# A gated convolution and token MLP on one Trainium2 core: kv transform with a butterfly over even and odd rows, halves in another order, more sums by accumulating DMAs

## Chip, core and metric

The kernel runs on one core of a Trainium2 chip. The metric is device time in microseconds (us). "Before" is the kernel without the change. Names of engines: TensorE (PE) does matmuls and writes PSUM; PEld in a profile is its weight loads. VectorE (DVE), ScalarE (ACT) and GpSimd (POOL) compute on SBUF; SyncE (SP) issues most DMAs, ACT issues four small ones and POOL the accumulating ones.

## The reference

Sequence length S = 2048, width D = 640, hidden width F = 1536, all bfloat16:

```python
x = A_q
g = sigmoid((x * gate_w).sum(-1, keepdims=True))
k_shift[s] = sum over t in 0..3 of k[s - 3 + t] * shift_k[:, 3 - t]
kv = k_shift * v
y = irfft(rfft(pad(kv)) * rfft(pad(ssm_k)))[:S] + kv * ssm_D     # causal convolution over s
a = q * y
h = layernorm(x over D)
u = gelu(einsum("sd,sf->df", h, w1) + b1)
b = (einsum("df,fs->ds", u, w2) + b2).T
out = g * a + (1 - g) * b
```

## The kernel before

**Convolution.** The sequence is cut into two halves of 1024 rows. ssm_k and kv are transformed half by half by matmuls against a table of sines and cosines, `FTB`. A half is split into four phases p (row = 4m + p), and each phase is a transform over 256 values of m, two blocks kt of 128 partitions. Its output has two frequency blocks k2 and two components c. `fwd` (line 832) does one phase: for each (k2, c) a group of four matmuls (two kt, two chunks ci of 320 columns) accumulates in PSUM, and ScalarE evicts 640 columns. `mixing` (846) joins the four phases with VectorE sums and differences. `C[0]` and `C[1]` hold the transforms of the two kernel halves (V0, V1 after `mixing` and `v1mix`), `C[2]` and `C[3]` those of kv (A0, A1). `cross` (1089) forms A0 times V1 in V1's place, `product` (1062) A0 times V0 and A1 times V0, `acc_dma` (1070) adds A0 V1 onto A1 V0. `invmix` (1104) undoes the mixing and `inverse(h, Z)` (1123) transforms back with the transposed table `GTB`, multiplies by the gate on eviction and by q on VectorE, adds the MLP's share in `O1` and stores.

**Rows.** ssm_k comes with the channel on the partitions and is turned by TensorE (`transp`, 818, one group per phase and kt). k is turned by a DMA transpose (`k_turn`); `kv` (949) does the 4-tap convolution as banded matmuls.

**MLP.** The first layer ("m1") is 12 tiles ft of 32 matmuls, in groups of 8 per 512 rows hk; its w1 chunks lie in `ring`. The second ("m2") is four blocks of 512 rows in the order `HORD` (1021), each with four groups of 24 matmuls; its `W2` tiles reuse the ring, two alternating, so a block's weights can be loaded only when the block before last is done.

**Order.** The code writes no order by hand. Every operation is handed to a planner (`_Sched.add`, 353) with an estimated duration and a priority (its index unless given); `run` (383) simulates the engines and picks, per engine, the ready operation with the smallest priority, and `emit` issues in that order. Convolution groups and MLP groups share four PSUM slots (at most three and two). m1 has priority 10^6 and up, m2 2x10^6, so MLP groups fill gaps. In `add`, what an evictor depends on is also made a dependence of its group's first matmul. Each engine and each DMA queue then runs its list in order, with semaphore waits where the tracker (`_Tracker`) finds an overlap in memory. The mixing of the kernel halves has priority `MIXP` = 330.

**Aliases that matter.** `wT` lies on C[2]; `ssm`, `vkv0` and `v1` on C[3]; `q_lo` on C[1] slots 2 and 3; `q_hi` on KF and its neighbours; `gq` (the gate's products) on GTB; `cgb` (the inverse's result) on FTB; `tm` and `kv1` on KT.

**End.** `cross(0)`, `cross(1)`, the products for the second half, `invmix`, `inverse(1)`; then a sign change of half of GTB (`neg`), the products of A0 and V0, `invmix`, `inverse(0)`. The last m2 group is joined to the output by VectorE straight from PSUM (`last_stt`).

## Time and profile before

| | us |
|---|---|
| median of 8 runs (lowest to highest) | 191.35 (191.03 to 192.12) |
| the profiled execution | 191.3 |
| its span, first to last instruction | 189.5 |
| 384 + 384 MLP matmuls of 320 columns, busy | 54.1 + 53.1 |
| 64 evictions of transforms (128x640), ScalarE | 39.6 |
| 12 accumulating DMAs on POOL's queue: 2752 packets, 6.55 MB | 20.2% of 16 DMA engines |
| all SP loads and stores: 34464 packets, 32.15 MB | 55.6% |

How to read it: times in the profile are from one execution; its span leaves out 1.8 us of the time measured for that execution. A matmul's profiled duration includes its way through the array, and consecutive ones overlap. A group line gives output and input tiles (buffer numbers left out), shapes, count, busy time and the mean of one in ns. Almost all TensorE, ScalarE and VectorE work has the line of a helper (293, 666, 622), so groups are told apart by tiles and shapes.

### The profile page before, as it was taken

The numbers are of one execution on the slowest core, as the hardware profiler recorded it, in microseconds if no ns is written. First come the engines' busy times: TensorE is split into PE (matmuls) and PEld (weight loads), VectorE is DVE, ScalarE is ACT, GpSimd is POOL, SyncE is SP. The second block draws the span as 40 slices with busy tenths as digits, with TensorE's granted clock in tenths as the row PEclk, the third lists the DMA queues.
The fourth block names the chain that finished last, engine by engine and source line by source line (L and its number), as shares of the span: only waits on it lengthen the run. The fifth ranks groups of instructions, "written<-read, shape, count | busy, mean of one in ns | idle before, by whom it ended". The sixth has DMA issues, their size and how long they took to land.

```text
span 189.5 us, 3367 instructions
## 1 busy us (share of the span) xinstructions
PE 176.5 (93%) x1403; PEld 131.7 (70%) x1403; DVE 170.8 (90%) x197; ACT 116.2 (61%) x185; POOL 33.4 (18%) x33
## 2 busy tenths in 40 slices
PE   0479998979999999999999999999999999999994
PEld 0446575648767886677777777888888777877783
DVE  7999968994999999999999999999999999994253
ACT  4997989899989999997412221131322487337430
POOL 2199021850004510000011303250000000000000
PEclk9999999999999999999999999999999999999999
DMA  4999999993999999996368954999947903400222
GB/s 152 393 394 347 393 237 218 309 401 135 132 191 359 224 156 183 297 317 198 72 142 230 238 100 150 274 208 191 263 136 234 368 16 134 142 2 0 73 104 104
DMA packets 37295, 38.93 MB, mean 205 GB/s; under 512 B 15643, under 2 KB 32672, under 8 KB 37280
## 3 DMA queue, kind: packets, MB, share of 16 engines
q1 hardware_dynamic: 34464, 32.15, 55.6%
q0 software_dynamic: 2752, 6.55, 20.2%
q8 instruction: 11, 0.18, 0.4%
q14 instruction: 4, 0.03, 0.0%
q10 hardware_dynamic: 64, 0.01, 0.0%
HBM read 25.87 MB, written 2.62 MB: 150 GB/s over the span
## 4 chain that ended last, share of the span: by engine, by line
PE 88%; ACT 8%; DMA 3%; issue 0%; DVE 0%
PE pp L293 88%; DMA ssm<-in_A_ssm_k_dram 3%; ACT C L666 3%; ACT wT L666 2%; ACT FTB L666 1%; ACT L666 1%; ACT cw L666 0%; ACT GT L666 0%; DVE O L678 0%
## 5 line engine op out<-in xcount | busy, mean ns | idle before, releaser
L293 PE MATMUL pp<-X,ring 128*128 128x320 bf16 x384 | 54.1, 299 | 0.0
L293 PE MATMUL pp<-GT,W 128*128 128x320 bf16 x384 | 53.1, 299 | 0.0
L293 PEld LDWEIGHTS pp<-GT,W 128*128 128x128 bf16 x384 | 43.6, 113 | 8.7
L622 DVE TENSOR_TENSOR C<-C 128x2560 bf16<-128x2560 bf16 (+1 forms) x28 | 48.9, 1770 | 0.0
L293 PEld LDWEIGHTS pp<-X,ring 128*128 128x128 bf16 x384 | 37.4, 98 | 14.4
L666 ACT ACTIVATE C<-pp 128x640 bf16<-128x640 f32 x64 | 39.6, 729 | 3.2 <-PE pp L293 3.2
L666 ACT ACTIVATE O<-pp,c,omg 128x640 bf16<-128x640 f32 x15 | 13.3, 884 | 27.7 <-PE pp L293 27.7
L262 POOL DMA_DIRECT2D C<-C x10 | 11.0, 1195 | 71.6 <-DVE C L622 40.2
L666 ACT ACTIVATE GT<-pp,cc 128x640 bf16<-128x640 f32 x12 | 9.6, 798 | 22.2 <-PE pp L293 22.1
L293 PE MATMUL pp<-wT,FTB 128*128 128x320 bf16 x128 | 20.2, 313 | 1.2 <-ACT C L666 1.1
L666 ACT ACTIVATE cgb<-pp,gg 128x640 bf16<-128x640 f32 x16 | 12.7, 794 | 11.1 <-PE pp L293 11.0
L293 PEld LDWEIGHTS pp<-wT,FTB 128*128 128x128 bf16 x128 | 11.7, 102 | 8.8 <-ACT C L666 3.3
L622 DVE TENSOR_TENSOR tm<-C,C 128x2560 bf16<-128x2560 bf16 (+1 forms) x8 | 16.9, 2148 | 0.0
L293 PE MATMUL pp<-ident,ssm 128*128 128x128 bf16 x80 | 8.3, 265 | 9.0 <-DMA ssm<-in_A_ssm_k_dram 7.2
L622 DVE TENSOR_TENSOR C<-tm 128x2560 bf16<-128x2560 bf16 (+1 forms) x12 | 14.9, 1263 | 0.1
L293 PEld LDWEIGHTS pp<-ident,ssm 128*128 128x128 bf16 x80 | 6.6, 128 | 10.6 <-DMA ssm<-in_A_ssm_k_dram 7.2
L293 PE MATMUL pp<-C,GTB 128*128 128x320 bf16 x96 | 13.9, 299 | 0.0
L876 DVE BATCH_NORM_STATS2 stats<-X 128x6 f32<-128x320 bf16 x32 | 13.3, 452 | 0.0
L666 ACT ACTIVATE gq<-gq 128x640 bf16<-128x640 bf16 x16 | 11.9, 763 | 0.4 <-DVE gq L622 0.4
L293 PEld LDWEIGHTS pp<-C,GTB 128*128 128x128 bf16 x96 | 9.0, 98 | 4.2 <-ACT O L666 0.3
L622 DVE TENSOR_TENSOR tm<-C,SS 128x5120 bf16<-128x5120 bf16 x4 | 11.2, 2817 | 0.0
L666 ACT ACTIVATE wT<-pp 128x640 bf16<-128x640 f32 x16 | 10.2, 710 | 0.6 <-PE pp L293 0.4
(65 smaller groups left out, 178.6 us busy)
## 6 DMA issues: line engine op xcount, KB each, us to landing
ring<-in_B_w_dram SPq DMA_DIRECT2D x12, 512.0 KB, 12.0
W<-in_B_w_dram SPq DMA_DIRECT2D x8, 768.0 KB, 7.0
C<-C POOLq DMA_DIRECT2D x6, 640.0 KB, 9.5
ssm<-in_A_ssm_k_dram SPq DMA_DIRECT2D x4, 640.0 KB, 9.5
X<-in_A_q_dram SPq DMA_DIRECT2D x4, 640.0 KB, 8.8
kn<-in_A_k_dram SPq DMA_DIRECT2D x4, 640.0 KB, 8.5
out_dram<-O SPq DMA_DIRECT2D x7, 320.0 KB, 2.3
vkv<-in_A_v_dram SPq DMA_DIRECT2D x2, 640.0 KB, 5.1
```

The costliest lines, as they stand in the source:

```text
L262: ins = engobj.dma_start(out_ap, in_ap, accum_op=ALU.add, max_dma_last_dim=2560)
L293: ins = self.nc.tensor.matmul(ps_ap, lhsT=lhsT, rhs=rhs, start=start, stop=stop, skip_group_check=True)
L622: o_ = SC.add(eng, d, lambda s: T.op(eng, lambda e: e.tensor_tensor(o, a, b, op), [a, b], [o]), [a, b], [o], prio=prio, name="tt")
L666: return T.op("ACT", lambda e: e.activation(o, src, func, **kw), rr + [src], ww)
L876: ops.append(SC.add("DVE", 0.38, (lambda o, i: lambda s: T.op("DVE", lambda e: e.bn_stats(o, i), [i], [o]))(o, i), [i], [o]))
```

## The change

**Rows and table.** k and v are loaded with row = 8q + 4kt + p in a half, so kt is the parity of m and no longer its block. The table's frequencies in block k2 = 1 are those of k2 = 0 shifted by 512. ssm_k is loaded in five DMAs by half and channel block (the whole first half ahead of X), and turned in groups of eight transposes per channel block, stride 8, evicted as 1024 columns.

**Even phases.** For kv's phases 0 and 2, `fwd_even` transforms even and odd rows apart, for k2 = 0 only, into a staging area (C[1] slots 0 and 1 for the first half, C[2] slots 0 and 1 for the second), and three VectorE operations form both frequency blocks as sums and differences.

**Sums by DMA.** In the second half's mixing one sum, in the products of A0 one sum each, and in the first half's inverse the four sums with `O1` are made by DMAs with an adding write, issued on POOL's queue.

**Order.** The half finished first is the first: HORD is (0, 1, 2, 3), and `inverse(0)` comes before `inverse(1)`. `q_hi` holds products' temporaries before it holds q. The transposed table is put back into FTB with even and odd rows interleaved (`gil`), the inverse reads it there, and `neg` is gone. Planner figures: the DMA rate goes from 320 to 365 (transposes of k from 170 to 200), a POOL-issued DMA's end is put 3 us later and its bytes halved, and the last m2 group no longer waits in the plan for what its evictor needs (`keep`).

```diff
-                    if d.vt is not vt:
+                    if d.vt is not vt and not vt.keep:
...
-                    op.end = dma_free + 2.0 + (3.0 if e == "POOL" else 0.0)
+                    op.end = dma_free + 2.0 + (6.0 if e == "POOL" else 0.0)
...
-        cgb = [alloc(f"cgb{i}", [128, 2, D], BF16, at=base_of(FTB) + 2560 * i) for i in range(3)]
+        cgb = [alloc(f"cgb{i}", [128, 2, D], BF16, at=base_of(GTB) + 2560 * i) for i in range(3)]
...
-        def ssm_load(hk):
-            dma(ssm[:, :, 512 * hk:512 * hk + 512], dr(A_ssm_k, 512 * hk, [[S, 128], [128 * S, ND], [1, 512]]), 128 * ND * 1024, chain=True)
+        def ssm_load(h, a, b):
+            dma(ssm[:, a:b, 1024 * h:1024 * h + 1024], dr(A_ssm_k, 128 * S * a + 1024 * h, [[S, 128], [128 * S, b - a], [1, 1024]]), 128 * (b - a) * 2048, chain=True)
+
+        def row8(t, hk):
+            return dr(t, (1024 * (hk // 2) + 4 * (hk % 2)) * D, [[8 * D, 128], [1, 4 * D]])
+
+        def kcol(hk):
+            return 16 + 128 * (1 - hk % 2)
...
-            dma(kn[hk % 2][:, :, :], dr(A_k, 512 * hk * D, [[4 * D, 128], [1, 4 * D]]), 128 * 5120, chain=True)
+            dma(kn[hk % 2][:, :, :], row8(A_k, hk), 128 * 5120, chain=True)
...
-            dma(dst, dr(A_v, 512 * hk * D, [[4 * D, 128], [1, 4 * D]]), 128 * 5120, chain=True)
+            dma(dst, row8(A_v, hk), 128 * 5120, chain=True)
...
+        SSM0 = ((0, 1), (1, 3), (3, 5))
+        SSM1 = ((0, 2), (2, 5))
...
-        ssm_load(0)
-        x_load(0)
-        ssm_load(1)
-        for hk in range(1, 4):
+        for a, b in SSM0:
+            ssm_load(0, a, b)
+        for hk in range(4):
             x_load(hk)
-        ssm_load(2)
-        ssm_load(3)
+        for a, b in SSM1:
+            ssm_load(1, a, b)
...
-        iota(acol[:, :, :], [[512, 2], [1, 4]], 0, 4)
-        iota(brow[:, :, :], [[2, 2], [4, 128]], 1, 0)
+        iota(acol[:, :, :], [[4, 2], [1, 4]], 0, 8)
+        iota(brow[:, :, :], [[-512, 2], [4, 128]], 1, 0)
...
-        def transp(h, p, kt):
+        def transp(h, db):
             vt = _VT("cv")
             items = []
-            hk = 2 * h + kt
-            dfold = hk == 0 and p == 0
-            if dfold:
-                for lo, hi in ((0, 512), (512, 640)):
-                    items.append(((lambda s, lo=lo, hi=hi: s[:, lo:hi]), ident[0:1, :], Drow[0:1, lo:hi], True, False))
-            for db in range(ND):
-                items.append(((lambda s, db=db: s[:, db * 128:db * 128 + 128]),
-                              V(ssm, db * S + 512 * hk + p, [[4, 128]]), ident[:, :], not dfold, True))
+            for kt in range(2):
+                for p in range(4):
+                    o = (lambda s, j=4 * kt + p: s[:, 128 * j:128 * j + 128])
+                    dfold = h == 0 and kt == 0 and p == 0
+                    if dfold:
+                        items.append((o, ident[0:1, :], Drow[0:1, 128 * db:128 * db + 128], True, False))
+                    items.append((o, V(ssm, db * S + 1024 * h + 4 * kt + p, [[8, 128]]), ident[:, :], not dfold, True))
             mms(vt, items, name="wtr")
-            act(wT[:, hk, p, :], full, ACT.Copy, vt=vt, name="wT")
+            act(V(wT, 2 * h * SL + 128 * db, [[SL, 2], [D, 4], [1, 128]]), (lambda s: s[:, :].rearrange("q (a b c) -> q a b c", a=2, b=4)), ACT.Copy, vt=vt, name="wT")
...
+        def fwd_even(src, h, dst, Th, Ts):
+            pos = {(0, 0, 0): 0, (0, 0, 1): 1, (0, 1, 0): 2, (0, 1, 1): 3, (2, 0, 1): 4, (2, 1, 0): 5, (2, 1, 1): 6, (2, 0, 0): 7}
+            for p in (0, 2):
+                for kt in range(2):
+                    for c in range(2):
+                        vt = _VT("cv")
+                        items = [(chk(ci), FTB[:, p, kt, c, 0, :], src(kt, p, ci), True, True) for ci in range(2)]
+                        mms(vt, items, name="A")
+                        act(V(Th, Ts * SL + D * pos[(p, kt, c)], [[320, 2], [1, 320]]), two, ACT.Copy, vt=vt, name="Ae")
+
+            def t4(o, n, dims):
+                return V(Th, Ts * SL + D * o, dims + [[1, n]])
+            tt_("DVE", V(dst, 0, [[2 * D, 2], [1, D]]), t4(0, 2 * D, []), t4(2, 2 * D, []), ALU.add)
+            tt_("DVE", V(dst, 2 * SL + 2 * D, [[-2 * D, 2], [1, D]]), t4(4, 2 * D, []), t4(6, 2 * D, []), ALU.add)
+            tt_("DVE", V(dst, D, [[2 * SL, 2], [2 * D, 2], [1, D]]), t4(0, D, [[4 * D, 2], [D, 2]]), t4(2, D, [[4 * D, 2], [D, 2]]), ALU.subtract)
...
-            for p in PORD:
-                for kt in range(2):
-                    transp(h, p, kt)
+            for db in range(ND):
+                transp(h, db)
...
-        for p in PORD:
-            fwd(lambda kt, p, ci: vkv0[:, kt, p, 320 * ci:320 * ci + 320], 0, p, C[2], p, 1.0, "A")
+        SC.add("POOL", 0.3, lambda s: T.op("POOL", lambda e: e.tensor_copy(KT[1][:, :, 15:16], KT[0][:, :, 143:144]), [KT[0][:, :, 143:144]], [KT[1][:, :, 15:16]]),
+               [KT[0][:, :, 143:144]], [KT[1][:, :, 15:16]])
+        srcA = lambda kt, p, ci: vkv0[:, kt, p, 320 * ci:320 * ci + 320]
+        fwd_even(srcA, 0, C[2], C[1], 0)
+        for p in (1, 3):
+            fwd(srcA, 0, p, C[2], p, 1.0, "A")
         mixing(C[2], C[1], 0)
         for hk in range(2, 4):
             kv(hk)
-        for p in PORD:
-            fwd(lambda kt, p, ci: kv1[:, kt, p, 320 * ci:320 * ci + 320], 1, p, C[3], p, 1.0, "A", lambda c, k2: k2 == 1)
-        mixing(C[3], C[2], 0)
+        srcB = lambda kt, p, ci: kv1[:, kt, p, 320 * ci:320 * ci + 320]
+        fwd_even(srcB, 1, C[3], C[2], 0)
+        for p in (1, 3):
+            fwd(srcB, 1, p, C[3], p, 1.0, "A")
+        def mixing_acc(R, Th, Ts):
+            def sl(h, s, n=1):
+                return V(h, s * SL, [[1, n * SL]])
+
+            def pr(h, s, rev=False):
+                return V(h, s * SL + (1280 if rev else 0), [[-1280 if rev else 1280, 2], [1, 1280]])
+            for i in range(2):
+                tt("DVE", sl(Th, Ts + i), sl(R, i), sl(R, 2 + i), ALU.subtract)
+                dma(pr(R, i), pr(R, 2 + i), 128 * 5120, stream="POOL", prio=0, accum=True)
+            tt("DVE", sl(R, 2), sl(R, 0), sl(R, 1), ALU.add)
+            tt("DVE", sl(R, 3), sl(R, 0), sl(R, 1), ALU.subtract)
+            tt("DVE", V(R, SL, [[-1280, 2], [1, 1280]]), pr(Th, Ts), pr(Th, Ts + 1, True), ALU.add)
+            tt("DVE", V(R, 0, [[3 * 1280, 2], [1, 1280]]), pr(Th, Ts), pr(Th, Ts + 1, True), ALU.subtract)
+
+        mixing_acc(C[3], C[2], 0)
...
-        HORD = (2, 3, 0, 1)
+            act(V(FTB, 1024 * p, [[1, 2], [256, 4], [2, 128]]), V(GTB, 1024 * p, [[512, 2], [128, 4], [1, 128]]), ACT.Copy, prio=10 ** 5, name="gil")
+
+        HORD = (0, 1, 2, 3)
         lastvt = []
-        for kt in range(2):
-            dma(q_hi[:, kt, :, :], dr(A_q, (1024 + 512 * kt) * D, [[4 * D, 128], [1, 4 * D]]), 128 * 5120)
         for n_, hk in enumerate(HORD):
             W2h = W2[n_ % 2]
...
+                        vt.keep = True
...
-        A1 = {0: (C[3], 2), 1: (C[2], 0)}
+        A1 = {0: (C[3], 2), 1: (C[3], 0)}
...
+        npr = [0]
+
+        def product(dst, a, v, late=False):
             tt("DVE", P2(T0), P2(a), P2(v), ALU.mult)
+            if late:
+                n_ = npr[0] % 2
+                npr[0] += 1
+                tt("DVE", V(q_hi, n_ * SL, [[1280, 2], [1, 1280]]), H(a, 1), H(v, 0), ALU.mult)
+                tt("DVE", H(dst, 1), H(a, 0), H(v, 1), ALU.mult)
+                tt("DVE", H(dst, 0), H(T0, 0), H(T0, 1), ALU.subtract)
+                dma(H(dst, 1), V(q_hi, n_ * SL, [[1280, 2], [1, 1280]]), 128 * 5120, stream="POOL", prio=0, accum=True)
+                return
...
-                tmp = V(C[3], 1280 * (n_ % 4), [[1, 1280]])
+                tmp = V(q_hi, 1280 * (n_ % 4), [[1, 1280]])
...
-                                items.append((chk(ci), GTB[:, p, kt, c, k2, :], V(hz, sz * SL + (2 * c + k2) * D + 320 * ci, [[1, 320]]),
+                                items.append((chk(ci), V(FTB, 1024 * p + 512 * c + 256 * k2 + 128 * kt, [[1, 128]]), V(hz, sz * SL + (2 * c + k2) * D + 320 * ci, [[1, 320]]),
...
+                qv = (q_hi if h == 0 else q_lo)[:, :, p, :]
+                tt("DVE", qv if h == 0 else cg[:, :, :], cg[:, :, :], qv, ALU.mult)
...
+                elif h == 0:
+                    dma(ov, qv, 128 * 2560, stream="POOL", prio=0, accum=True)
+                    dma(dr(out, (1024 * h + p) * D, [[4 * D, 128], [512 * D, 2], [1, D]]), ov, 256 * 1280, sem="out")
...
-        cross(0)
-        cross(1)
-        y1(0)
-        y1(1)
-        Z1 = invmix(A1[0], A1[1], C3a, None, None)
+        for g in range(2):
+            cross(g)
+        for g in range(2):
+            product(A0[g], A0[g], V0[g], True)
+        for kt in range(2):
+            dma(q_hi[:, kt, :, :], dr(A_q, 512 * kt * D, [[4 * D, 128], [1, 4 * D]]), 128 * 5120)
+        for g in range(2):
+            product(A1[g], A1[g], V0[g])
+            acc_dma(A1[g], V1[g])
+        for kt in range(2):
+            dma(q_lo[:, kt, :, :], dr(A_q, (1024 + 512 * kt) * D, [[4 * D, 128], [1, 4 * D]]), 128 * 5120).after.add(w2last)
+        Z0 = invmix(A0[0], A0[1], C3a, None, None)
+        inverse(0, Z0)
+        Z1 = invmix(A1[0], A1[1], (SS, 0), None, None)
         inverse(1, Z1)
-        for p in (0, 2, 1, 3):
-            gk = GTB[:, p, :, :, 1, :]
-            act(gk, gk, ACT.Copy, scale=-1.0, name="neg")
-        for kt in range(2):
-            dma(q_lo[:, kt, :, :], dr(A_q, 512 * kt * D, [[4 * D, 128], [1, 4 * D]]), 128 * 5120).after.add(w2last)
-        product(A0[0], A0[0], V0[0])
-        product(A0[1], A0[1], V0[1])
-        Z0 = invmix(A0[0], A0[1], (SS, 0), None, None)
-        inverse(0, Z0)
```

## The prediction

> **What bounds the kernel now.** I read the busy shares first, then the chain that ended last in order of time, then a table of busy time by stage, then the two busiest engines as timelines. The shares leave two candidates:
>
> ```profile
> PE 176.5 (93%) x1403; PEld 131.7 (70%) x1403; DVE 170.8 (90%) x197; ACT 116.2 (61%) x185; POOL 33.4 (18%) x33
> ```
>
> The chain decides between them. Its last pieces (start, length, what); the two before them are TensorE from 42.03 and 0.03 of issue:
>
> ```profile
> 46.42 19.40 PE pp L293 x192
> 65.82 0.03 issue
> 65.84 89.23 PE pp L293 x680
> 155.07 0.01 issue
> 155.08 31.74 PE pp L293 x232
> 186.82 0.02 issue
> 186.84 0.55 DVE O L678
> ```
>
> From 42 us to 186.8 us TensorE never waits, so the end is set by the sum of its matmuls. How near VectorE is shows by stage (first length, then busy PE, PEld, DVE, ACT, POOL, clock, DMA share, GB/s):
>
> ```profile
> 14.50:43.20 28.70, 26.95 (x203) 17.45 (x202) 26.21 (x54) 26.09 (x43) 13.18 (x9) 1.00 1.04 319
> 43.20:83.20 40.00, 39.95 (x395) 29.96 (x393) 36.69 (x28) 38.40 (x68) 5.10 (x4) 1.00 1.00 211
> 83.20:116.90 33.70, 33.70 (x251) 24.29 (x249) 33.67 (x33) 11.84 (x24) 3.46 (x4) 1.00 0.67 167
> 116.90:148.40 31.50, 31.50 (x235) 26.31 (x233) 31.43 (x17) 8.76 (x10) 4.87 (x4) 1.00 0.93 232
> ...
> 170.50:187.00 16.50, 16.30 (x121) 12.65 (x118) 7.06 (x12) 7.42 (x9) 0.00 (x0) 1.00 0.19 67
> ```
>
> The clock is full throughout. VectorE is full from 43 to 170.5 us, so it is the second bound, but it ends early. The timelines, VectorE's last butterflies first and then TensorE after them, show by how much:
>
> ```profile
> 167.67 2.89 DVE L622 TENSOR_TENSOR SS<-C,C 128x2560 bf16<-128x2560 bf16 x2
> ```
>
> ```profile
> 171.43 2.34 PE L293 MATMUL pp<-SS,GTB 128*128 128x320 bf16 x16
> 173.60 3.42 PE L293 MATMUL pp<-GT,W 128*128 128x320 bf16 x24
> 176.86 2.34 PE L293 MATMUL pp<-SS,GTB 128*128 128x320 bf16 x16
> 179.03 7.77 PE L293 MATMUL pp<-GT,W 128*128 128x320 bf16 x56
> ```
>
> When VectorE has finished the last butterflies (about 170.5), TensorE still has 80 MLP matmuls that need nothing more from it.
>
> **Matmuls removed.** In each half, `fwd` for phases 0 and 2 issues 2 x 4 groups x 4 = 32 matmuls; `fwd_even` issues 8 groups x 2 = 16. Two halves lose 32. The profiled mean of 299 ns is latency, not pace. The pace is start to start: 28 kv-transform matmuls begin at 52.78 and the next group at 56.62, 3.84/28 = 137 ns; 248 matmuls from 83.19 to 116.88 give 136 ns. 32 x 0.1365 = **4.37 us**, inside the stretch that sets the end. ScalarE evicts 8 groups of 640 columns as before, so it gains nothing; it is 96% busy from 43.2 to 83.2, and TensorE stays dense there only because MLP matmuls fill in. By 83 us, 17 of the 48 first-layer groups of 8 are done and 31 are left, so filler does not run out.
>
> **A new wait.** `fwd_even` parks its partial sums in C[1] slots 0 and 1 (first half) and C[2] slots 0 and 1 (second). So even-phase evictions can start only when mixing of C[1] ends (64.1 us in the trace), and then that of C[2] (80.7). Before, the first half's transform began at 52.78. Queued behind on TensorE: nothing if the planner knows the wait, and it does, because an evictor's dependences are passed to the group's first matmul. In that gap TensorE can do the odd phases (32 x 0.137 = 4.4), the second half's convolution (4.3) and MLP groups at 1.09 each, 10 us of cover for 52.8 to about 62.5. VectorE waits for 8 evictions at about 0.61 (7 in 4.28), 4.9 us, less the two kv products and gate products that fit there: 0 to 3 us lost, I take 1.5. Those are VectorE's, not yet TensorE's.
>
> **VectorE.** Steps by start: 1.40 for 128x2560 (34.69 to 37.50 for two), 2.74 for 128x5120, 0.74 for 128x1280. Added: two butterflies of 2 x 0.74 + 1.40 = 5.8. Removed: one 5120 sum in the second mixing, with the 5120 difference becoming two of 2560 (-2.7); in each product of A0, one 5120 product becomes two of 2560 (+0.06) and one 2560 sum goes (-2.7 for two); four 1280 sums of the inverse (-3.0). Net -2.6: the last butterflies would end near 168, with the new wait 169.5, while TensorE ends at 186.8 - 4.4 = 182.4. After them TensorE needs at least 32 inverse matmuls (4.4), so VectorE can lose 182.4 - 4.4 - 169.5 = 8.5 us more before TensorE stands idle.
>
> **Eight more accumulating DMAs**: two of mixing, two of the A0 products (655 KB each), four in the inverse (328 KB each), 3.9 MB. Nearest rows (KB each, us to landing):
>
> ```profile
> W<-in_B_w_dram SPq DMA_DIRECT2D x8, 768.0 KB, 7.0
> C<-C POOLq DMA_DIRECT2D x6, 640.0 KB, 9.5
> ...
> C<-SS POOLq DMA_DIRECT2D x2, 640.0 KB, 16.2
> ```
>
> So 9.5 to 16.2 us late; I take 10. After the two mixing sums VectorE has the rest of `cross` (four rounds of about 3.6 us) and two products (7 us each) to do, over 20 us; after the products, those of A1 (16 us). Both cover 16. The inverse's sums go to the half finished first, and its stores sit on SP behind them, some 15 us before the end. Here a rule speaks against: the Trainium skill ("SBUF — State Buffer", "A bandwidth-pool intuition that's wrong") says GpSimd can't write descriptors while VectorE holds the shared port: 620 ns become 3100. If that came on top, each pair of sums would land 5 us later, at 15 to 21 instead of 10 to 16, and the mixing pair would just come out from under its cover: some 1 us of VectorE, still inside its slack, 187.0 either way, but a second pair late by as much would be rival (b). The rows were mostly taken beside a full VectorE (33.67 of 33.70 us), so they hold that wait already. I go by the rows: 0.
>
> **Kernel transposes.** Same 80, now with a stride of 8 elements (16 bytes) in the stationary operand instead of 4, and evicted as 10 of 1024 columns instead of 16 of 640. Row: 15 weight loads in 0.97 us, 65 ns each. The same page ("Door 1: The DMA port swizzle") says SBUF lines are 16 bytes and an access in a new line each time pays. By the row it costs 0, a sum of 187.0; by the rule, if the load doubles, 80 x 65 ns = 5.2 us of TensorE and at most 192.2, of which the stage up to 43.2 has room for most (28.7 us, with 158 x 0.1365 + 45 x 0.065 = 24.5 of pace in them). A gain is not excluded (fewer evictions: the 128x1024 form takes 1.035 against 0.710, so 10.4 against 11.4), and the first load is 262 KB instead of 655 KB, 1 us earlier at 393 GB/s. Against it: no kernel transform can begin before all five groups of its half are evicted, where it began after two: some 0.7 us of ScalarE bubble per half. And X lands up to 1.6 us later, behind the first half's 1.31 MB, in front of a VectorE that is busy until 8. Sum of this stage: -1.5 to +2, I take 0.
>
> **The rest, at nothing.** `gil`: four 128x1024 copies, nearest row 1.14 each, 4.6 on ScalarE after 93 us, against 2.5 for `neg` removed; ScalarE then waits 2.4 to 3.6 us at a time for TensorE. Without that cover 4.6. The q load of the half finished first moves on SP from 67.7 us to behind the A0 products' DMAs: W2 loads, the second q load and stores stand behind it. If it waits too long, the second MLP layer waits for W2. `keep` and HORD move only groups that are ready; planner figures cost no time themselves.
>
> **Sum.** Profiled execution 191.3 (span 189.5 and 1.8 around it), median 191.35: the same within 0.05. 191.35 - 4.37 + 0 = **187.0 us**.
>
> **Rivals.** (a) W2 is late. A block of the second layer runs 4 x 24 x 0.136 = 13.0 us, and its W2 loads can be issued only when the block before last is done. They land in 4.4 to 10.2 now, with DMA at 0.93. The layer gets two 655 KB sums and two q loads (2.6 MB) more. For: ring loads beside four accumulating DMAs took 15.1 us. Against: SP's ring loads there stood behind the q loads. Three loads count: at 14.5 us each the gain is gone (3 x 1.5 = 4.4), above 14.7 it is slower; at 15.5, 7.4 lost, 194.4. This is the case on the other side. (b) VectorE becomes the bound: the mixing sums land at 16 with the order planned for 11, twice, and the even-phase wait is 3 instead of 1.5: up to 12 us late, 3.5 beyond the slack of 8.5, and a longer tail: 189 to 191. For: it has under 1% idle. Against: the cover above. (c) The saved matmuls leave holes, since ScalarE sets the pace of the transforms: 191.3. For: 96% ScalarE. Against: 31 groups of filler. (d) The start gains too: 185.5.
>
> **How the numbers follow.** 187.0 (186 to 188.3): 0.60. (d), under 186: 0.05. Part of (a), (b) or the transposes' rule, 188.3 to 190.7: 0.15. Within 0.3% of 191.35 (190.8 to 191.9, about what these runs can tell from no change), (c): 0.06. Slower, (a) in full: 0.14. So faster 0.80, same 0.06, slower 0.14. Leaving out the 0.14, 0.04 at the top of (c) and 0.02 at the bottom of (d): 185.2 to 191.0.
>
> **What would show it.** 32 fewer 320-column matmuls; TensorE without gaps from 43 us to its end at about 182.4; VectorE's last butterflies near 168 to 170 with MLP matmuls left; even-phase evictions after 62 us. Wrong would be: TensorE waiting for W2 after 112 us, VectorE waiting for a POOL-queue DMA by over 8.5 us in all, weight loads of the transposes at 130 ns each, or gaps between 50 and 85 us that a C[1] or C[2] eviction ends.

## The result and the profile after

The changed kernel takes **189.97 us** (median of 11 executions, 189.52 to 190.66) against 191.44 (32 executions of the kernel before on the same chips): a ratio of 0.9921, 95% interval 0.9905 to 0.9938. It is 1.5 us faster where 4.4 were forecast. The direction was right, and the time lies in the range (185.2 to 191.0). Ratios here leave out executions more than 1.5% above the fastest of their kernel; a median named beside one can still contain some.

The lines that answer to those shown of before. Busy shares of the changed kernel:

```profile
PE 173.5 (92%) x1374; PEld 129.5 (69%) x1374; DVE 168.7 (90%) x199; ACT 119.3 (64%) x180; POOL 50.2 (27%) x41
```

TensorE is busy for 3.0 us less, VectorE for 2.1 (forecast: 2.6). The end of its chain (start, length, what):

```profile
92.58 0.02 issue
92.60 1.30 ACT C L667 x2
93.90 0.10 ACT gth L667
94.00 1.80 ACT C L667 x3
95.80 1.24 ACT FTB L667
97.05 0.65 ACT GT L667
97.69 0.14 issue
97.83 87.29 PE pp L293 x640
185.12 0.02 issue
185.14 0.55 DVE O L679
```

Before, the chain was TensorE alone from 42 us on. Now it is TensorE alone only from 97.83; ahead of that it runs through ScalarE: evictions, then a copy into FTB (`gil`), then a GELU. TensorE ends at 185.12 instead of 186.82: 1.70 earlier, not 4.4. By stage (first, length, then PE, PEld, DVE, ACT, POOL, clock, DMA share, GB/s):

```profile
14.50:43.20 28.70, 26.25 (x198) 17.79 (x199) 26.16 (x60) 23.70 (x35) 17.86 (x10) 1.00 1.09 328
43.20:83.20 40.00, 39.85 (x392) 29.93 (x391) 32.20 (x25) 38.09 (x68) 9.24 (x5) 1.00 0.97 213
83.20:116.90 33.70, 32.51 (x240) 23.43 (x239) 33.28 (x36) 20.86 (x35) 5.90 (x6) 1.00 0.77 153
116.90:148.40 31.50, 31.50 (x234) 26.28 (x233) 31.47 (x18) 8.36 (x10) 4.83 (x4) 1.00 0.81 230
...
170.50:187.00 16.50, 14.60 (x107) 10.36 (x105) 13.76 (x16) 7.44 (x10) 0.63 (x1) 1.00 0.63 187
```

TensorE has lost 1.2 us in the stretch 83.2 to 116.9, where it was full before. VectorE went from 36.69 to 32.20 in the stretch 43.2 to 83.2, and from 7.06 to 13.76 in the last: it runs late. VectorE's last butterflies, then TensorE's last pieces:

```profile
173.87 2.89 DVE L623 TENSOR_TENSOR SS<-C 128x2560 bf16<-128x2560 bf16 x2
```

```profile
172.87 4.58 PE L293 MATMUL pp<-C,FTB 128*128 128x320 bf16 x32
177.28 4.51 PE L293 MATMUL pp<-SS,FTB 128*128 128x320 bf16 x32
181.65 3.45 PE L293 MATMUL pp<-GT,W 128*128 128x320 bf16 x24
```

The butterflies end at 176.8 instead of the 169.5 of the forecast, and 24 MLP matmuls (3.3 us) are left after that, all behind the last inverse, where there were 80.

**Where the 4.37 us went.** TensorE's idle time is each matmul's start to the next one's start, less the pace of its columns (back to back, both traces show 0.136 us for 320 columns and 0.056 for 128; others by the line through the two), summed by stage in both traces. The first transform matmuls, which start 0.267 us apart (some 9 before, 15 after), count in part as idle. Stages are cut at the same work: the first transform matmul, the start of the kv transforms' stretch (44.3 before, 48.5 after), its end (83.2 and 97.8).

| | before | after | difference |
|---|---|---|---|
| first transform matmul starts at | 14.55 | 16.34 | +1.79 |
| idle from there to 44.3 / 48.5 | 4.66 | 3.89 | -0.77 |
| idle from there to 83.2 / 97.8 | 0.63 | 2.30 | +1.67 |
| idle after | 0.38 | 0.35 | -0.03 |
| 32 matmuls of 0.1365 | | | -4.37 |
| sum | | | -1.71 |
| TensorE's end | 186.82 | 185.12 | -1.70 |

So the saved matmuls are there in full. They were eaten by a later start (1.0 us net of the idle time behind it) and by holes, stretches in which TensorE stands idle, among the kv transforms (1.7). The experiments take these one by one.

### The profile page after: what moved, and what is told of

Same layout as the page of the kernel before. It is cut to its first block, busy times and chain, and to the rows that moved or that the text cites. A ratio compares the mean times of both kernels' runs of the same rounds, so it can differ in the third digit from the quotient of the medians.

```text
span 187.8 us, 3316 instructions
## 1 busy us (share of the span) xinstructions
PE 173.5 (92%) x1374; PEld 129.5 (69%) x1374; DVE 168.7 (90%) x199; ACT 119.3 (64%) x180; POOL 50.2 (27%) x41
## 4 chain that ended last, share of the span: by engine, by line
PE 81%; ACT 15%; DMA 2%; issue 1%; DVE 0%
PE pp L293 81%; ACT C L667 4%; ACT wT L667 4%; ACT FTB L667 3%; ACT ksh L667 2%; DMA ssm<-in_A_ssm_k_dram 2%; ACT L667 1%; ACT GT L667 1%; ACT cw L667 0%; DVE O L679 0%; ACT gth L667 0%
## 5 line engine op out<-in xcount | busy, mean ns | idle before, releaser
L623 DVE TENSOR_TENSOR C<-C 128x2560 bf16<-128x2560 bf16 (+2 forms) x34 | 52.2, 1563 | 6.6 <-ACT C L667 6.6
L293 PE MATMUL pp<-X,ring 128*128 128x320 bf16 x384 | 55.4, 299 | 1.5 <-ACT GT L667 1.2
L293 PEld LDWEIGHTS pp<-X,ring 128*128 128x128 bf16 x384 | 37.2, 98 | 16.5 <-issue 1.9
L262 POOL DMA_DIRECT2D C<-q_hi x6 | 5.9, 984 | 54.5 <-DVE C L623 27.5
L262 POOL DMA_DIRECT2D C<-C x8 | 9.9, 1359 | 33.3 <-DVE C L623 33.1
L623 DVE TENSOR_TENSOR tm<-C,C 128x2560 bf16<-128x2560 bf16 (+1 forms) x7 | 14.4, 2054 | 0.0
L996 POOL COPY KT<-KT 128x20 bf16<-128x20 bf16 x1 | 13.6, 13582 | 2.7 <-DMA KT<-kp 2.7
L293 PE MATMUL pp<-C,FTB 128*128 128x320 bf16 x96 | 13.7, 299 | 0.0
L623 DVE TENSOR_TENSOR SS<-C 128x2560 bf16<-128x2560 bf16 x8 | 11.6, 1486 | 0.9 <-DMA C<-C 0.9
L623 DVE TENSOR_TENSOR C<-tm 128x2560 bf16<-128x2560 bf16 (+1 forms) x10 | 12.0, 1218 | 0.0
L293 PEld LDWEIGHTS pp<-C,FTB 128*128 128x128 bf16 x96 | 8.9, 98 | 4.2 <-ACT O L667 0.4
```

Of the source, the lines that this page charges most:

```text
L262: ins = engobj.dma_start(out_ap, in_ap, accum_op=ALU.add, max_dma_last_dim=2560)
L293: ins = self.nc.tensor.matmul(ps_ap, lhsT=lhsT, rhs=rhs, start=start, stop=stop, skip_group_check=True)
L623: o_ = SC.add(eng, d, lambda s: T.op(eng, lambda e: e.tensor_tensor(o, a, b, op), [a, b], [o]), [a, b], [o], prio=prio, name="tt")
L996: SC.add("POOL", 0.3, lambda s: T.op("POOL", lambda e: e.tensor_copy(KT[1][:, :, 15:16], KT[0][:, :, 143:144]), [KT[0][:, :, 143:144]], [K ...
```

## The start: Sins behind a copy

ScalarE at the start, before and then after:

```profile
2.33 1.28 ACT L666 ACT_TABLE_LOAD   x1 [2.33 <-issue]
4.11 2.19 ACT L666 ACTIVATE FTB<-pint,cst 128x1024 bf16<-128x1024 int32 x2 [0.50 <-DVE pint L636]
6.42 1.30 ACT L666 ACTIVATE wT<-pp 128x640 bf16<-128x640 f32 x2
```

```profile
2.31 1.28 ACT L667 ACT_TABLE_LOAD   x1 [2.31 <-issue]
4.97 1.02 ACT L667 ACTIVATE wT<-pp 128x1024 bf16<-128x1024 f32 x1 [1.38 <-PE pp L293]
6.01 1.28 ACT L667 ACT_TABLE_LOAD   x1
7.31 2.20 ACT L667 ACTIVATE FTB<-pint,cst 128x1024 bf16<-128x1024 int32 x2
```

Before, the first activation is a Sin, and one table load at 2.33 serves it and the copies behind it. After, a `wT` copy comes first; a second load of 1.28 us stands between it and the first Sin, and the Sins start 3.2 us later. All later `wT` copies shift with them, and the first transform matmul waits for the last. Two ways to mend it. A tiny Sin first, with the order of the rest kept:

```diff
         memset("DVE", cst[:, 1:2], -0.5)
+        act(gws[:, :], cst[:, 1:2], ACT.Sin, name="warm")
```

> The changed kernel with one tiny Sin activation put first on ScalarE, every other instruction in the same order. Theory (the changed order lets a Copy run before the first Sin, so ScalarE loads a second table of 1.28 us at 6.0 us, and all that follows it in the start waits): two table loads instead of three, the first kernel-transform matmul near 15.1 instead of 16.34, time 1.0 to 1.3 us below the changed kernel's 189.97, some 188.8. Rival (the start was bound by loads or by the eight-fold groups' evictions, the table load lay in time nobody waited for): no change beyond 0.3 us.

Measured: 189.46 us, ratio 0.9876 (0.9843 to 0.991). The second load is gone, but the first Sin still stands behind a `wT` copy (it runs at 5.88), and in the profile the second part of ssm_k landed only at 7.02, so that the first transform matmul started at 16.51. A gain of 0.45% whose interval overlaps that of the changed kernel: in part right, not settled. The other way puts the first two Sins ahead of the copies:

```diff
         PORD = (0, 2, 1, 3)
+        sins = []
...
-            act(FTB[:, p, :, :, :, :].rearrange("q a b c d -> q (a b c d)"), pa, ACT.Sin, bias=cst[:, 0:1],
-                scale=-(2.0 * math.pi / 4096.0) * (1.0 - 1e-6), name="sin")
+            sins.append(act(FTB[:, p, :, :, :, :].rearrange("q a b c d -> q (a b c d)"), pa, ACT.Sin, bias=cst[:, 0:1],
+                scale=-(2.0 * math.pi / 4096.0) * (1.0 - 1e-6), name="sin"))
...
-(lambda s: s[:, :].rearrange("q (a b c) -> q a b c", a=2, b=4)), ACT.Copy, vt=vt, name="wT")
+(lambda s: s[:, :].rearrange("q (a b c) -> q a b c", a=2, b=4)), ACT.Copy, vt=vt, name="wT").after.update(sins[:2])
```

> The changed kernel with the evictions of the turned kernel made to follow the first two Sin activations, as they did before. With Sin first only one table is loaded ahead of it, and Sin runs while the second ssm_k load is still on its way. Theory of the start (1.3 us of table load and the Sin work behind it move the whole start, and every later stage with it): two table loads, first kernel-transform matmul at 15.0 to 15.4 instead of 16.34, last butterflies of VectorE near 175.5 instead of 176.8, time 0.9 to 1.4 us under the changed kernel. Rival (the load landing sets it, 5.6 to 7.0 us from run to run, as in the run with one tiny Sin first): less than 0.4 us under it.

It ran beside the changed kernel itself:

> The changed kernel itself, beside the next three on the same chip, so that differences of half a per cent can be read. Both theories expect the ratio of 0.992 to the kernel before, within 0.002.

Measured: the changed kernel 190.12 (0.9921, 0.9892 to 0.995, as before); the Sins ahead **188.24**, ratio 0.9825 (0.9806 to 0.9843). ScalarE's start and TensorE's of that kernel:

```profile
4.10 2.20 ACT L667 ACTIVATE FTB<-pint,cst 128x1024 bf16<-128x1024 int32 x2 [0.51 <-DVE pint L637]
```

```profile
14.64 5.78 PE L293 MATMUL pp<-wT,FTB 128*128 128x320 bf16 x21 [1.44 <-ACT wT L667]
```

The Sins start where they did before, and the first transform matmul at 14.64 instead of 16.34. Part of this is the load: the second part of ssm_k landed at 5.90 here, at 6.64 in the changed kernel. With the Sins ahead, the first transform matmul follows that landing by 8.7 us in all eleven traces with this edit (14.6 to 15.9); in the seven traces without it, it comes at 16.1 to 16.5, with landings from 5.6 to 7.0. The edit takes ScalarE's order off the path and leaves the load on it. Nor do all of the 1.7 us last: some 20 matmuls instead of 15 start 0.267 us apart, and by the end of the first kv convolution 1.1 us are left (TensorE goes on at 51.83 instead of 52.93). With 0.4 us less idle from 44 to 98 us, where the planner, with everything earlier, no longer put a copy in front of a GELU at 96 us, TensorE ends 1.5 us earlier in this trace. Repeated:

> The Sins ahead alone, once more: 188.24 plus or minus 0.5, ratio 0.980 to 0.986.

Measured: 188.75, ratio 0.9817 (0.9752 to 0.9882), four executions. In its trace the second part of ssm_k landed at 6.90 and the first transform matmul came at 15.63, and TensorE still goes on at 51.84. No version was clearly faster than this one.

## The copies that were costed at nothing

ScalarE and TensorE of the changed kernel around the one hole in the kv stretch that is over 0.3 us:

```profile
95.69 1.36 ACT L667 ACTIVATE FTB<-GTB 128x1024 bf16<-128x1024 bf16 x1
96.90 0.78 ACT L667 ACTIVATE GT<-pp,cc 128x640 bf16<-128x640 f32 x1
```

```profile
97.83 17.55 PE L293 MATMUL pp<-X,ring 128*128 128x320 bf16 x128 [1.19 <-ACT GT L667]
```

The second `gil` copy runs while a finished MLP group waits for its GELU, and TensorE waits for the PSUM slot. The edit moves the copies behind the last GELU:

```diff
-[[512, 2], [128, 4], [1, 128]]), ACT.Copy, prio=10 ** 5, name="gil")
+[[512, 2], [128, 4], [1, 128]]), ACT.Copy, prio=10 ** 5, name="gil").after.add(g_)
```

> The changed kernel with the four interleaving copies of the table made to follow the last GELU in the plan. Theory (a copy of 1.36 us at 95.7 on ScalarE stands in front of a GELU eviction for which TensorE waits 1.19 us at 96.6): that gap goes, time 0.9 to 1.3 us below 189.97, some 188.9. Rival (the gap is made by the second half's even-phase evictions, which are late whatever the copies do): the gap stays at about 1 us or comes back next to it, no change beyond 0.3 us. A third: VectorE, which ends its last butterflies only at 176.8, has become the bound, and TensorE's earlier filler turns into a wait before the last inverse: no change either, but with a gap near 177.

Measured: 189.87, ratio 0.9892 (0.9864 to 0.9919). The hole at 96 us shrinks from 1.35 us of lost pace to 0.33, but the time falls by 0.3%, and the intervals overlap. The trace shows where the gain went. VectorE still ends its last butterflies at 176.8, and the MLP matmuls behind the last inverse are 12 instead of 24. TensorE's last piece and VectorE's:

```profile
182.53 1.79 PE L293 MATMUL pp<-GT,W 128*128 128x320 bf16 x12
```

```profile
185.24 1.01 DVE L679 SCALAR_TENSOR_TENSOR O<-pp,omg,cgb 128x320 bf16<-128x320 f32 x2
```

TensorE ends at 184.3, 0.8 us earlier than in the changed kernel, but the last inverse ends 0.9 us later (182.53 instead of 181.65), and the way from it to the output (an eviction, then VectorE's products and sums) takes 2.7 us and ends last. In the changed kernel the two met: VectorE waits 0.17 us for TensorE before its last piece. So filling the hole alone gains next to nothing in this order. That is near the third case of the expectation, but at the end of the kernel and not as a gap near 177. With both edits:

> Two edits of the changed kernel together: the Sins ahead of the wT copies, and the four gil copies behind the last GELU. Theory (losses add where each leaves a hole in TensorE; with the Sins ahead the hole at 96 us is gone already, and 24 MLP matmuls are left behind the last inverse): nothing more to be had from gil, 188.2 (ratio .982 to .985), TensorE's end within 0.4 us of the 183.6 that the Sins ahead alone gave. Rival (the two gains add, 1.9 and 0.3 us or more): under 187.8, ratio under .981. Rival on the other side (the table put back late keeps the first inverse waiting): above 188.8.

Measured: 188.48, ratio 0.9842 (0.9801 to 0.9883), TensorE without a hole over 0.4 us from 40 us on. Nothing more than with the Sins ahead alone, as the first theory had it.

## What the butterfly is worth

The butterfly undone in the changed kernel (all four phases of kv by the full transform):

```diff
-        fwd_even(srcA, 0, C[2], C[1], 0)
-        for p in (1, 3):
+        for p in PORD:
             fwd(srcA, 0, p, C[2], p, 1.0, "A")
...
-        fwd_even(srcB, 1, C[3], C[2], 0)
-        for p in (1, 3):
+        for p in PORD:
             fwd(srcB, 1, p, C[3], p, 1.0, "A")
```

> The changed kernel with kv's phases 0 and 2 transformed as phases 1 and 3 are (32 matmuls more, no staging, six VectorE operations fewer), all else kept. Theory (the removed matmuls are worth their 4.37 us where TensorE never waits, less the gaps of 1.7 us between 48 and 98 us that staging brought): 2.7 to 4.4 us above 189.97, 192.7 to 194.4, and VectorE's last butterflies at 166 to 171 instead of 176.8. Rival (the butterflies gave back all that the matmuls saved, since VectorE and ScalarE set the pace): within 1 us of 189.97.

Measured: 197.03, ratio 1.0255 (1.0223 to 1.0287), 6.4 us more than the changed kernel (0.0334 x 191.4). That refutes the rival that the butterfly gave its gain back, but 6.4 is not 4.37. The same with the Sins ahead:

> The Sins ahead and the butterfly undone (all four phases of kv by the full transform), so that the butterfly's worth is seen in a plan without the start's loss: to compare with the Sins ahead alone (188.24). Theory 1 (the butterfly is worth its matmuls, 32 x 0.1365 = 4.37, once TensorE has no holes; the 6.5 measured in the changed kernel had 2 us of holes in it): 192.2 to 193.0, ratio 1.004 to 1.008. Theory 2 (its matmuls and 2 us of ScalarE's pace): 194.3 to 195, ratio 1.014 to 1.019. Rival (the full transform has cover, and half of it is hidden): under 191.4.

Measured: 196.57, ratio 1.0269 (1.0232 to 1.0305): 8.5 us over the Sins ahead alone. More still, and none of the theories. The trace names it. TensorE, and ScalarE ahead of it, in this kernel:

```profile
107.17 14.89 PE L293 MATMUL pp<-X,ring 128*128 128x320 bf16 x96 [3.06 <-ACT GT L667]
```

```profile
105.14 1.35 ACT L667 ACTIVATE FTB<-GTB 128x1024 bf16<-128x1024 bf16 x1 [4.62 <-DMA GTB<-FTB]
106.35 0.77 ACT L667 ACTIVATE GT<-pp,cc 128x640 bf16<-128x640 f32 x1
```

A `gil` copy is in front of a GELU again, and here it waits for its DMA transpose, which lands 6.6 to 13.0 us after its issue; in the changed kernel the same four take 3.2 (median). With only the copies moved behind the last GELU:

> The Sins ahead, the butterfly undone, the four gil copies behind the last GELU. Theory 1 (the butterfly is worth its matmuls, 4.37, and what it cost more was the copies ahead of a GELU): no hole over 1 us at 100 to 110 us, 192.4 to 193.6, ratio 1.005 to 1.011, that is 4.2 to 5 over its control. Theory 2 (2 us more in ScalarE's pace): 194.5 to 196, ratio 1.016 to 1.024. Rival (the transposes beside the sums now delay W2): a hole that ends with a W2 load, over 196.

Measured: **192.0**, ratio 1.0035 (1.0007 to 1.0063), 4.6 us less, and no hole over 1 us. Against the same two edits with the butterfly (0.9842) it is 3.7 us, against the Sins ahead alone 4.0, with some 1 us of uncertainty: the butterfly is worth its 32 matmuls, less about 0.5 to 0.8 us of small holes that it brings (idle from 44 to 98 us: 1.61 and 1.89 with it, 1.10 without). The 8.5 was that and the copies. Of the 6.4 without the Sins ahead, the trace shows 1.2 us in more small holes from 44 to 98 us (3.53 against 2.30), 0.4 behind a copy at 108 and 1.0 at 169.6, where TensorE waits for VectorE; these were not taken apart.

## The sums by DMA

All eight of the added accumulating DMAs made into VectorE additions:

```diff
-                dma(pr(R, i), pr(R, 2 + i), 128 * 5120, stream="POOL", prio=0, accum=True)
+                tt("DVE", pr(R, i), pr(R, i), pr(R, 2 + i), ALU.add)
...
-                dma(H(dst, 1), V(q_hi, n_ * SL, [[1280, 2], [1, 1280]]), 128 * 5120, stream="POOL", prio=0, accum=True)
+                tt("DVE", H(dst, 1), H(dst, 1), V(q_hi, n_ * SL, [[1280, 2], [1, 1280]]), ALU.add)
...
-                    dma(ov, qv, 128 * 2560, stream="POOL", prio=0, accum=True)
+                    tt("DVE", ov, qv, ov, ALU.add)
```

> The changed kernel with the eight added DMA sums made by VectorE again (two sums of 2560 columns in the mixing, two in the products, four of 1280 in the inverse: 4 x 1.40 + 4 x 0.74 = 8.6 us). Theory (VectorE has only some 3 us of slack left, 24 MLP matmuls after the last inverse): last butterflies near 185, TensorE waits for them, time 5 to 9 us above 189.97. Rival of the forecast (VectorE has 8.5 us of slack, so the DMA sums are not needed for the time): less than 1 us above.

Measured: 196.23, ratio 1.0235 (1.0201 to 1.0268), 6.0 us over the changed kernel. In the profiled execution (198.88) VectorE's last butterflies end at about 184.0, 7.2 later, and TensorE stands:

```profile
179.78 7.28 PE L293 MATMUL pp<-C,FTB 128*128 128x320 bf16 x32 [3.29 <-DVE C L623]
186.90 4.51 PE L293 MATMUL pp<-SS,FTB 128*128 128x320 bf16 x32
```

Nothing is left behind the last inverse. With 8.6 us more work on VectorE for 6.0 us of time, VectorE's slack in the changed kernel was at most 2.6 us and not 8.5, and the DMA sums are needed.

Another wait has come closer. The changed kernel was profiled twice, and in the second trace (190.24 us) its chain runs through an accumulating DMA that is none of the eight. It belongs to the two pairs that add A0 V1 onto A1 V0 (`acc_dma`). The kernel before has them too, issued by 126 us, ahead of the half that comes first; with the halves in the other order they are issued at 143.6 to 154.0 and stand ahead of the last butterflies:

```profile
154.01 14.29 DMA C<-C
168.39 1.49 DVE SS L623
...
170.62 2.82 DVE C L623 x2
173.57 12.21 PE pp L293 x88
```

This one was under way for 14.3 us. VectorE waited 1.26 and 1.27 us for the two pairs, and TensorE 0.53 us for VectorE; it ends at 185.8 instead of 185.1. In the first trace the same waits of VectorE are 0.59 and 0.29 us and TensorE has none.

## Waiting for the staging area

In the changed kernel VectorE waits 2.57 and 1.58 us for even-phase evictions of the first half, which wait for C[1]:

```profile
72.07 0.83 DVE L623 TENSOR_TENSOR C<-C 128x1280 bf16<-128x1280 bf16 x1 [2.57 <-ACT C L667]
74.47 2.23 DVE L623 TENSOR_TENSOR C<-C 128x1280 bf16<-128x1280 bf16 x2 [1.58 <-ACT C L667]
```

Does this lateness cost time? First the staging area was laid on a ring buffer, whose w1 loads then had to come later:

```diff
-        for hk in range(4):
-            w1_load(1, hk)
...
-        fwd_even(srcA, 0, C[2], C[1], 0)
+        fwd_even(srcA, 0, C[2], ring[1], 0)
         for p in (1, 3):
             fwd(srcA, 0, p, C[2], p, 1.0, "A")
+        for hk in range(4):
+            w1_load(1, hk)
```

> The changed kernel with the first half's even-phase sums parked in the second ring buffer instead of C[1], and that buffer's w1 load issued after them, so that their evictions no longer wait for the mixing of C[1]. Theory (VectorE became the second bound: it stands still for 4.9 us between 66 and 77 us for these evictions, and its last butterflies end at 176.8 where 169.5 was forecast): the waits at 69 to 75 us go, last butterflies at 172 to 174, and more than 24 MLP matmuls are left after the last inverse; the time itself falls only by what holes on TensorE go with it, 0 to 1 us. Rival (TensorE lacks filler when w1 comes later): a gap of TensorE near 70 us that a ring load ends, and no gain or a loss.

> The three together: Sin ahead, interleaving copies after the last GELU, staging in the ring buffer. Theory (TensorE's holes of 1.8 us at the start and 1.2 us near 96 us are the missing part of the forecast gain, and without VectorE's lateness they can be had): TensorE ends near 182.5, time 186.8 to 187.8, ratio to the kernel before 0.976 to 0.981. Rival (each hole closed opens another one, since ScalarE and VectorE are as full as TensorE): ratio above 0.986.

Measured: 198.13, ratio 1.0317 (1.0277 to 1.0356), and with the Sins ahead and late copies 195.4, 1.0134 (1.0084 to 1.0184). The rival won: the waits at 69 to 75 us are gone, but TensorE's filler waits for its weights, as in the first of these kernels:

```profile
83.47 1.26 PE L293 MATMUL pp<-X,ring 128*128 128x320 bf16 x8 [2.66 <-DMA ring<-in_B_w_dram]
...
87.26 6.20 PE L293 MATMUL pp<-X,ring 128*128 128x320 bf16 x32 [1.98 <-DMA ring<-in_B_w_dram]
```

Then it was laid on tiles 4 to 11 of GT, with the Sins ahead, and no load moved:

```diff
-        fwd_even(srcA, 0, C[2], C[1], 0)
+        fwd_even(srcA, 0, C[2], GT, 1)
```

> The Sins ahead, and the staging area of the first half laid on GT tiles 4 to 11 (free then but for the shifted k of the second half) in place of C[1], so that no even-phase eviction waits for a mixing and no weight load moves. Theory 1 (with the start mended TensorE alone sets the end; VectorE's wait is under cover): VectorE's staging waits of some 4 us between 69 and 75 us go, its last butterflies end at 171 to 173 instead of 174.8, more MLP matmuls stand behind the last inverse (40 or more), and the time stays at 188.2 plus or minus 0.4. Theory 2 (VectorE is the co-bound still): 186.0 to 187.5. Rival (the second half's shifted k, kept off GT, comes later and delays its transform by as much): VectorE's butterflies not earlier than 174.8, 188 to 190.

> All three: Sins ahead, staging on GT, gil behind the last GELU. Theory 1: 188.0 plus or minus 0.4, no better than the best of the others by more than 0.3. Theory 2: 0.3 to 1 us under the staging on GT alone. If the copies, now late, keep the first inverse waiting: above it.

Measured: 202.42, ratio 1.0539 (1.0475 to 1.0604); with late copies 189.96 to 199.46 from execution to execution, so no ratio. None of the theories again. The wait is gone (the first butterfly runs at 57.9, in the changed kernel at 72.07), but the transposes of the table into GTB came too late: GTB holds the gate's products until 94 us there. SyncE, ScalarE and TensorE of the first of the two:

```profile
91.22 3.49 SPq L260 DMA_TRANSPOSE GTB<-FTB  x2
94.76 0.59 SPq L267 DMA_DIRECT2D W<-in_B_w_dram  x1
95.39 13.20 SPq L260 DMA_TRANSPOSE GTB<-FTB  x2
```

```profile
112.49 1.35 ACT L667 ACTIVATE FTB<-GTB 128x1024 bf16<-128x1024 bf16 x1 [13.46 <-DMA GTB<-FTB]
113.71 0.77 ACT L667 ACTIVATE GT<-pp,cc 128x640 bf16<-128x640 f32 x1
```

```profile
114.53 11.53 PE L293 MATMUL pp<-X,ring 128*128 128x320 bf16 x64 [9.64 <-ACT GT L667]
```

Two transposes, issued beside the accumulating DMAs of `cross` and the mixing (POOL issues at 94.9, 96.3, 97.9 and 102.6), take 13.2 us to issue. A copy waits for them in front of a GELU, and TensorE waits for the GELU. With late copies TensorE waits instead for W2, whose loads stand behind the transposes on SyncE (7.24 us at 123.5). To take the collision out, the transposes were put behind the last GELU, with the GT staging, with the C[1] staging and without the butterfly:

```diff
-128 * 2048, rate=200.0, transpose=True, prio=10 ** 5)
+128 * 2048, rate=200.0, transpose=True, prio=10 ** 5).after.add(g_)
```

> Sins ahead, staging on GT tiles, and the four transposes of the table into GTB (with the copies that follow them) put behind the last GELU, so that they stand neither ahead of a GELU nor ahead of the first W2 loads. If the collision of the transposes was what cost the two kernels before 8 to 14 us: no hole over 1 us in TensorE between 98 and 130 us, granted clock 1.0, 185.8 to 188.3. Theory 1 (TensorE alone sets the end once the start is mended) 187.4 to 188.3; theory 2 (VectorE's lateness still cost something) 185.8 to 187.3. Rival (the transposes now keep W2 loads of the third block waiting): a hole with a W2 load as its end at 138 to 142 us, 189 to 193.

> The Sins ahead and the transposes and copies behind the last GELU, staging on C[1] as in the changed kernel: the control for the run with staging on GT. There the transposes landed in 3.2 us and nothing waited for them, so nothing is to be gained: 188.2 plus or minus 0.5. Rival (W2 loads behind the transposes): above 189.

> The Sins ahead, the butterfly undone, transposes and copies behind the last GELU: to compare with its control. The butterfly's worth without the collision: theory 1 (its matmuls alone, 4.37) 192.2 to 193.0; theory 2 (over 2 us more, through ScalarE's pace or VectorE) 194 to 196.5; rival (part of it hidden) under 191.8.

Measured: 192.88 (1.0043, 1.0007 to 1.0079); 190.85 (0.9921, 0.989 to 0.9952); 234.84 (1.226, 1.2201 to 1.232). The expectations failed: this place has accumulating DMAs too, and the transposes land in 7.0, 7.2 and 31.1 us (medians). The copies now stand ahead of evictions of the second MLP layer, and TensorE has a hole of 3 us in the first two and of 12, 7 and 20 in the third. Yet the traces of the first two (193.52 and 193.82 us) answer the question, since they share the hole and differ in VectorE. Its last butterflies, GT staging first:

```profile
171.70 2.89 DVE L623 TENSOR_TENSOR SS<-C 128x2560 bf16<-128x2560 bf16 x2
```

```profile
177.33 2.89 DVE L623 TENSOR_TENSOR SS<-C 128x2560 bf16<-128x2560 bf16 x2
```

VectorE is 5.6 us earlier and 56 MLP matmuls stand behind the last inverse instead of 24, yet TensorE ends at 188.9 against 189.2, and by its ratio the kernel as a whole is 1.2% slower; why is not shown. Even with the later VectorE TensorE has no hole over 0.3 us after 130. In these two VectorE's lateness is under cover. (The 0.3 is no exact price: the GT staging has 1 us more of small holes between 44 and 98 us, 2.63 against 1.59, and the other's granted clock is lower behind the hole, 0.57 against 0.79 from 128 to 136 us.) It is cover without a margin: the late copies alone and the second trace of the changed kernel show VectorE setting the end as soon as the last inverse or a DMA ahead of it comes later.

## Why the prediction was right in direction and wrong in size

**Matmuls removed, 4.37:** right. TensorE's account shows it, and the butterfly undone with mended start and late copies costs 3.7 to 4.0.

**"Sum of this stage: -1.5 to +2, I take 0"** failed first; the term is +1.8 at the first transform matmul, +1.0 by the end of the stage. None of the listed items caused it. The working weighed shapes, loads and bubbles and did not ask in which order ScalarE would take the first copy and the first Sin. (That the copy came ahead because its load is smaller now is argued, not shown.) The Sins ahead won back 1.88 us, with the load's landing left on the path. What part the second table load has in it and what part the order was not separated. The bubble that I feared did not show: idle of the stage fell by 0.77.

**"`gil`: ... ScalarE then waits 2.4 to 3.6 us at a time for TensorE"** failed second. The copies (1.36 us each, against 1.14 by the row) run at 88.2, 95.7 and 99.3 to 101.9, before that cover begins: ScalarE's waits of 3.55 us start only after 103. I read the cover from the trace of before, where the kv transforms end at 83; after, they end near 99. One copy cost 1.2 us of hole, 1.35 of pace. "Without that cover 4.6" was too low a price as well: a copy that itself waits for a transpose passed on waits of 3 to 20 us.

**The new wait, "I take 1.5"**, was 2.57 and 1.58, and VectorE ended 7.3 us later than forecast (176.8 for 169.5) with the late start. **"VectorE can lose 8.5 us more"** was mis-sized too. The sum counts the 32 inverse matmuls (4.4) but not the way from the last of them to the last output, 181.65 to 184.42, 2.8 us. With TensorE's real end, 185.1 - 4.4 - 2.8 - 169.5 = 8.4, of which 7.3 were used: about 1 us was left (the sums put back on VectorE allow 2.6 at most). In the first trace that was enough (0.35 us of idle after 98), and making VectorE 5.6 us earlier bought at most 0.3. Rival (b) did not happen in the forecast's size, but its mechanism did: in the second trace TensorE waits 0.53 us for VectorE, which waited for a DMA, and with the copies late VectorE's last pieces set the end.

**Sums by DMA at 0:** right for the eight added ones. Those of 655 KB landed in 5.7 to 8.1 us (I took 10), those of 328 KB in 4.9 to 5.9, and VectorE waits for none of them. The waits of 0.59 and 0.29 us, 2.5 in the second trace, are for the `acc_dma` pairs that the order of the halves moved; the order I had put at nothing. W2 loads land in 7.1 as before (7.0) and nothing waits for them: rival (a) does not show in the time, nor the rule on the shared port in the issues of the sums (0.98 to 1.45 us each, by kind, beside a full VectorE). **Kernel transposes at 0:** right, 66 ns per weight load (24 in 1.58 us) against 65.

What is left: with the Sins ahead, 188.0 (0.9825 x 191.35) against the forecast 187.0. Its idle from 44 to 98 us is 1.89 instead of 0.63, three holes of 0.3 to 0.4 and many smaller ones; that is about the size of what is missing. Why these are there was not taken apart further.

## What to carry to other kernels

When a change alters when data arrives, ask which instruction moves to the front of each in-order queue, and what the queue pays for it: here putting the first Sins back ahead of the copies gave 1.9 us, more than a third of the forecast gain. Cover for a moved operation must be read where it will lie after the change, not in the trace of before; and an operation in an in-order queue is priced at its own length plus the longest wait of what it depends on. The slack of the second engine is counted to the last output, with the way that the first engine's results still have to go; when it is used up, a saving on the first engine alone gains nothing.

## What the runs showed that was not expected

**DMA transposes beside accumulating DMAs.** Four transposes of the table land in 3.2 us (median) in the changed kernel, where POOL issues no accumulating DMA between 68 and 95 us; 9.8 and 10.7 in two of the kernels that issue such DMAs beside them, 31.1 in the slowest. No run takes these DMAs away and leaves the rest, so that they are the cause is likely and not shown. DMA transposes in the changed kernel and in the one with GT staging (issue to landing, last figure):

```profile
GTB<-FTB SPq DMA_TRANSPOSE x4, 3.2
```

```profile
GTB<-FTB SPq DMA_TRANSPOSE x4, 10.7
```

**A hole costs twice.** After the hole of 9.64 us the granted clock (third figure from the end) was at half for 5.5 us; two stretches of the kernel with GT staging and early copies:

```profile
114.50:120.00 5.50, 5.47 (x21) 3.15 (x22) 5.50 (x5) 1.99 (x2) 1.20 (x1) 0.50 0.42 139
120.00:126.00 6.00, 6.00 (x46) 4.33 (x44) 6.00 (x3) 0.79 (x1) 0.00 (x0) 1.00 0.72 140
```

The 64 matmuls from 114.53 to 125.89 took 11.36 us where 64 x 0.1365 is 8.74: 2.6 us more lost. The Trainium skill ("TensorE: Matmul & The Clock Gate", "What's actually happening") puts the fall at one idle window of about 3.4 us; here, in the kernel without the butterfly and with early copies, the stretch from 104 to 114.5 us around a hole of 3.06 us already has a mean granted clock of 0.84, and in the ring-buffer kernel with all three edits a hole of 2.25 us (to 82.85) is followed by 0.50 from 84 to 87 us.

**Copies on POOL.** One KT copy took 13.58 us, 6.45 in the kernel before. VectorE was busy all along beside both, so the cause stays open. Nothing waited for it.
